# A planner's numbers and 73 of its ranks changed in a chunked-attention, Fourier-mix and MLP kernel; the instructions stay

## The chip, the cores and the metric

The kernel runs on one core of a Trainium2 chip, in one launch. The metric is device microseconds of the whole execution. Before the change the median of three runs is 278.01 us (277.71 to 278.85). The profile is one execution on the same core, read from a hardware trace.

## The reference, cut to what matters

Two parts follow each other. The first is attention in chunks of 32 queries: each chunk sees 8 memory keys, 16 keys to its left, its own 32 and 8 to its right. The second takes the attention's output as rows of 512, adds to each batch the real part of its two-dimensional Fourier transform, normalises the rows, and runs a two-layer MLP over them.

```python
batch, n_heads, seq, head_dim = (4, 8, 768, 64); chunk, left_ctx, right_ctx = (32, 16, 8); n_mem = 8
for c in range(nc):
    k_full = np.concatenate([mem_k, k_ctx], axis=2); v_full = np.concatenate([mem_v, v_ctx], axis=2)
    scores = scale * np.matmul(q_c, k_full.transpose(0, 1, 3, 2))
    a = softmax(scores)
    out[:, :, c_start:c_end] = np.matmul(a, v_full)
...
X = np.fft.fft(np.fft.fft(x, axis=1), axis=2)
u = x + np.real(X)
un = (u - mu) / np.sqrt(var + 1e-06)
ch = np.maximum(un @ w_ch1, 0.0) @ w_ch2          # 512 -> 2048 -> 512
return u + ch
```

## The kernel before, in words

The work is cut into 1,074 tasks. A task is a handful of instructions of one engine: one load, one group of matmuls, one vector operation. Nothing is emitted while the tasks are made. `plan.add` (a method of the class `Plan`) writes down each task's engine, an assumed cost, the tasks it comes after, the buffers it takes and gives back (`take`, `give`), and a rank. Then `plan.order` plays the whole program through as a list scheduler: at each moment each engine gets the ready task of lowest rank. The order in which tasks are placed is the order in which they are emitted, and so the order of every engine's queue on the chip. An engine works through its queue in that order: a task that isn't ready holds all those behind it.

The sixteen units of attention are numbered n = 0 to 15, four per batch, each a pair of heads. A unit loads q and k on GpSimd's DMA queue (`e_load_qk`, line 381 for the first twelve units and line 377 for the last four) and v on SyncE's (`e_load_v`, lines 390, 394 and 399, six DMAs). v is spread into overlapping windows, so its transfers are made of pieces of 256 bytes. Then come the transposes of q and k on TensorE (line 409, "trq" and "trk"), their copies to SBUF (`e_qT` on ScalarE, line 427; `e_kT`, line 452), the scores (line 465, in units 8 and up line 488), the exponentials on ScalarE (lines 475 and 500), the product with v (`e_values`, line 517, "xa" and "xo") and the division on VectorE (`e_norm`, lines 527 and 528). Before v of units 0 to 3 may be loaded, `e_edge_ones` (lines 354 to 359, GpSimd) has to set the edges of its buffer. The transposes need the identity matrix, made on GpSimd (masks.py) and cast on VectorE by `e_idb` (lines 1000 to 1003).

Batch 0 is transformed by `first_fourier` (tasks `g_...`; `g_rows` at line 748, `g_row` at 735), the others by `fourier` (line 589). After them `columns_of` makes the second half of the transform (lines 759 and 780), the sum, the statistics and the normalised rows. The last stage, the MLP, has its first layer at line 897 ("ph"), its relu at 906 and its second layer at 915 (plain form) or 964 (a form with seven products in place of eight, whose partial results VectorE reads at line 969 and whose inputs it combines at line 952). MLP tasks have ranks above 1,000,000: TensorE takes them when nothing else is ready. Task 93, `e_gate` (line 1081), is a one-element copy on GpSimd that waits for v of unit 3; the loads of unit 4 and later stand behind it.

While the first batch is waited for, the planner fills TensorE's gaps with dummy matmuls (line 1024, "idle"): they start once the first scores are placed and end with task 129.

For transfers the planner keeps a model of its own (`share`): a transfer begins `cost * head` after its issue, has a length `moved`, shares the DMA engines with the other queue by the weights `grain`, and its data count as there some time after it ends (`late` and a constant per queue). SyncE places no further task while more than `ROOM` is in its queue. Before the change, the order is the best of 24 plans whose ranks get random additions (`shortest`); tasks below `plan.lead` = 219, which are the first batch's, keep theirs.

Each tile's tag with its `bufs` is a ring of buffers: `rs` (line 857 ff., roots of the variance for the fast form) and `rstd` (line 878 ff., for the plain form) share the ring `rs` of two.

Of the kernel before, what the change touches and what calls it, by code (L numbers as in the profile page):

```python
# [37 lines left out]
class Plan:  # L38
# [10 lines left out]
    ROOM = 2.2  # L49
# [7 lines left out]
    def add(self, engine, cost, emit, after=(), take=(), give=(), rank=None, moved=0.0,  # L57
            loose=False, late=0.0, filler=False, behind=None, lag=0.0, pick=None, grain=0.1, head=1.0):
        t = dict(engine=engine, cost=cost, emit=emit, after=[a for a in after if a is not None],
                 take=take, give=give, rank=len(self.tasks) if rank is None else rank,  # L60
                 moved=moved, done=None, at=None, no=len(self.tasks), loose=loose,
                 late=late, filler=filler, behind=behind, lag=lag, picks=[pick] if pick else [], grain=grain, head=head)
        self.tasks.append(t)
        return t

    def share(self, now):

        left = {q: [list(x) for x in xs_] for q, xs_ in self.flow.items()}
        at = self.seen
        while any(left.values()):  # L70
# [3 lines left out]
            slow = {q: 0.85 if len(live) > 1 and xs_ and xs_[0][0]["grain"] < 0.05 else 1.0  # L74
# [5 lines left out]
            at += step  # L80
            for q, xs_ in left.items():
                if xs_ and xs_[0][2] <= at - step + 1e-9:
                    xs_[0][1] -= step * slow[q] * xs_[0][0]["grain"] / whole
            for q, xs_ in left.items():
# [11 lines left out]
    def shortest(self, tries, spread):  # L96

        free, ranks = dict(self.free), [t["rank"] for t in self.tasks]
        found = None
        for i in list(range(tries)) + [None]:  # L100
            draw = random.Random(found[1] if i is None else i)
            even = (found[1] if i is None else i) == 0
            self.free = dict(free)
            for t, rank in zip(self.tasks, ranks):
                move = draw.gauss(0.0, spread)
                t["rank"] = rank if even or rank < self.lead or rank > 1e5 else rank + move
                t["done"] = t["at"] = None
                for pick in t["picks"]:
                    pick.pop("tag", None)
            placed = self.order()  # L110
            if found is None or self.end < found[0]:
                found = (self.end, i)
        return placed

    def order(self):
        now, idle = 0.0, {}
        self.flow, self.seen, self.full = {}, 0.0, None
# [7 lines left out]
        while any(waiting.values()):  # L125
# [5 lines left out]
            for e, ts_ in waiting.items():  # L131
                if idle.get(e, 0.0) > now or (e == "SP" and self.full and self.full["done"] - self.ROOM > now):
                    continue
                held = False
                for t in ts_:
# [31 lines left out]
                    if t["moved"]:  # L167
# [3 lines left out]
                        if e == "SP" and t["moved"] > 2.5:  # L171
                            self.full = t
# [19 lines left out]
            if not moved:  # L192
# [3 lines left out]
                         + ([self.full["done"] - self.ROOM] if self.full else [])  # L196
# [10 lines left out]
def kernel(  # L207
# [669 lines left out]
    def e_rstd(b):  # L877
        rstd_of[b] = rstd = fpool.tile([P, NST], FP32, tag="rs", bufs=2, name="rstd")
# [116 lines left out]
    t_mkf = add("ACT", 0.2, e_mkf, moved=0.8)  # L995
# [64 lines left out]
    t_gate, LATE, t_flip = None, 1.0, [None]  # L1060
# [4 lines left out]
    def attention(n):  # L1065
# [5 lines left out]
                      take=(("qs", "ks")[i],), moved=3.1 if b >= TURNED else 1.2, grain=0.032 if b >= TURNED else 0.1, late=LATE if b else 2.0,  # L1071
# [4 lines left out]
                 take=("va",), moved=2.6, grain=0.031, head=0.4, late=(0.0, 4.0, LATE, LATE)[b])  # L1076
# [144 lines left out]
    def weights(n):  # L1221
        if n == HP + 1:
            t_w1.extend(add("POOL", 0.7, lambda dt=dt: nc.gpsimd.dma_start(
                w1_sb[:, dt, :], moe_w_ch1[ts(dt, P), :]), moved=2.4, grain=0.32, late=2.0,
                behind=t_mark[0], rank=t_ck[n]["rank"] + 0.1) for dt in range(NDT))
            t_ck[n] = t_w1[-1]
        else:
            t_w2.extend(add("POOL", 0.7, lambda g=g: nc.gpsimd.dma_start(
                w2_sb[:, ts(g, 4), :], w2v[:, ts(g, 4), :]), moved=2.6, late=2.0,
                behind=t_ck[n], rank=t_ck[n]["rank"] + 0.1) for g in (0, 2, 1, 3))  # L1230

    def first_fourier():
        t_rest, t_mid, t_row, pre = {}, {}, {}, {}
        for g in range(2):
            for par in range(2):
                zy = add("DVE", 0.5, lambda par=par, g=g: g_zy(par, g),
                         [t_norm[0, g], t_norm[1, g], t_sines],
                         take=("dn",) if (par, g) == (0, 0) else ())
                if g == 1:
                    w_ = add("DVE", 0.52, lambda par=par: g_w(par), [zy, t_norm[3, 1], pre[par, 1, 0]])  # L1240
# [5 lines left out]
                for ab in range(2):  # L1246
                    pre[par, ab, g] = add("DVE", 0.5,
                                          lambda par=par, ab=ab, g=g: g_ff(par, ab, g, 0),
                                          [zy, t_norm[2, g]],
# [13 lines left out]
            for par in range(2):  # L1263
                for ab in range(2):
# [5 lines left out]
                    else:  # L1270
                        ff = add("DVE", 0.55, lambda par=par, ab=ab: g_both(par, ab),
                                 pre[par, ab, 1][:2], give=("dn",) if (par, ab) == (1, 1) else ())
                    if (par, ab, g) == (0, 0, 1):
# [4 lines left out]
                    lo = add("DVE", 0.48, lambda par=par, ab=ab, g=g: g_lo(par, ab, g), [hi],  # L1278
                             give=("fold",) if end else ())
                    if (par, ab, g) == (0, 0, 0):  # L1280
# [5 lines left out]
                             [lo, t_neg] + ([t_row[g]] if mid_ else []),  # L1286
                             take=(tag,) if g == 0 and not mid_ else (),
                             give=(("hl",), ("hT",))[par] if end else ())
                    if g == 1:
# [8 lines left out]
    def fourier(b):  # L1298
        t_x1 = add("POOL", 1.0, lambda: e_rows_out(b), [t_norm[b * HP + i, 1] for i in range(HP)],
                   moved=2.0)  # L1300
        t_x2[b] = add("SP", 0.6, lambda: e_rows_turn(b), [t_x1], moved=5.5, grain=0.013, loose=True)
        t_xr[b] = add("POOL", 1.0, lambda: e_mirror(b), [t_x2[b]], take=("dn",), moved=2.0, grain=0.16)
# [3 lines left out]
        ff = hi = None  # L1306
        for par in range(2):
# [8 lines left out]
            for ab in range(2):  # L1316
# [5 lines left out]
                lo = add("DVE", 0.96, lambda par=par, ab=ab: e_lo(b, par, ab), [hi],  # L1322
# [269 lines left out]
```

## Time and profile before

| what | value |
|---|---|
| median of 3 runs | 278.01 us |
| span of the profiled execution | 275.7 us |
| its own time less its span | not shown separately; the median is 2.3 us above the span |
| TensorE busy (matmuls) | 258.7 us, 94% of the span |
| VectorE / ScalarE / GpSimd busy | 204.9 / 160.6 / 78.5 us |
| DMA moved | 39.98 MB, mean 145 GB/s |
| granted TensorE clock | 1.000 throughout |

The page gives busy time per engine and a strip of 40 slices of 6.9 us each, with tenths of busy time. A row of the timeline has a start, a duration, the engine, the line, the operation, output and inputs, and a count where like instructions follow each other; in square brackets stands the idle time of the engine just ahead of it and what ended that. Rows of stretches give for each engine the busy time in it, and the busy share of the DMA engines. Dummy matmuls count as busy.

### The profile page before, as it was taken

To read this page: it belongs to the slowest core of one execution; us is meant where nothing else is said; L and a number is where in the kernel's file an instruction comes from. 1 tells how busy PE (TensorE), PEld (TensorE's weight loads), DVE (VectorE), ACT (ScalarE), POOL (GpSimd) and SP (SyncE) were. 2 spreads that over 40 slices of the span, in tenths; PEclk is the share of its full clock that TensorE was granted. 3 is DMA by queue.
4 is the path that set the end of the run, shared out by engine and by line. 5 is a ranking of instruction groups with operands and counts; after the bars stand their busy time and mean duration, and the time that the engine had idled before them with its cause. 6 is when DMAs were issued, how large, how long until landed. Compare 5 with 4: busy or idle time off the path is not lost.

```text
span 275.7 us, 8160 instructions
## 1 busy us (share of the span) xinstructions
PE 258.7 (94%) x3365; PEld 209.8 (76%) x3365; DVE 204.9 (74%) x460; ACT 160.6 (58%) x300; POOL 78.5 (28%) x146
## 2 busy tenths in 40 slices
PE   0489999999999999999999989999999998999995
PEld 0367797888756788658669868888889887888884
DVE  7978999840337999998995997839997996354444
ACT  6888647888555688277646627555373483615150
POOL 8852652350111054045046246001100371000000
PEclk9999999999999999999999999999999999999999
DMA  6999999999997979958989964644960424313152
GB/s 104 203 176 176 193 211 205 198 195 200 174 190 176 204 170 175 212 79 160 241 144 199 183 118 117 123 117 146 132 182 1 95 62 83 111 40 76 64 90 76
DMA packets 116118, 39.98 MB, mean 145 GB/s; under 512 B 104561, under 2 KB 111473, under 8 KB 116081
## 3 DMA queue, kind: packets, MB, share of 16 engines
q1 hardware_dynamic: 93888, 23.54, 47.4%
q0 software_dynamic: 21472, 15.21, 34.8%
q10 hardware_dynamic: 720, 0.72, 0.8%
q8 instruction: 26, 0.43, 0.7%
q14 instruction: 12, 0.09, 0.1%
HBM read 37.36 MB, written 13.37 MB: 184 GB/s over the span
## 4 chain that ended last, share of the span: by engine, by line
PE 80%; DVE 11%; POOL 4%; ACT 2%; issue 1%; POOLq 0%; DVEq 0%
PE ph L897 26%; PE pc L964 14%; PE pc L915 10%; PE ps L589 6%; PE xa L517 5%; PE xo L517 4%; PE pm L759 3%; PE ps L748 3%; DVE S L952 2%; PE sc L465 2%; DVE st L832 2%; DVE xsb L969 2%; PE trk L409 2%; PE idle L1024 1%; PE trq L409 1%; DVE hT L952 1%
## 5 line engine op out<-in xcount | busy, mean ns | idle before, releaser
L897 PE MATMUL ph<-unT,w_sb 128*128 128x256 f16 x768 | 89.6, 273 | 0.0
L897 PEld LDWEIGHTS <-w_sb 128*128 128x128 f16 x768 | 73.7, 98 | 9.3 <-issue 0.3
L906 ACT ACTIVATE hT<-ph 128x512 f16<-128x512 f32 x96 | 56.3, 600 | 39.9 <-PE ph L897 21.1
L964 PEld LDWEIGHTS <-hT 128*128 128x128 f16 x320 | 30.8, 98 | 7.1 <-issue 2.0
L964 PE MATMUL pc<-w_sb,hT 128*128 128x256 f16 x256 | 32.1, 273 | 1.3 <-DVE xsb L969 0.9
L969 DVE TENSOR_TENSOR xsb<-pc,xsb 128x256 f32<-128x256 f32 x57 | 23.7, 420 | 12.6 <-PE pc L964 10.8
L915 PE MATMUL pc<-w_sb,hT 128*128 128x512 f16 x128 | 29.8, 380 | 0.0
L500 ACT ACTIVATE e<-sc,mbias 128x192 f32<-128x192 f32 (+1 forms) x48 | 19.2, 489 | 8.8 <-PE sc L488 8.8
L915 PEld LDWEIGHTS <-hT 128*128 128x128 f16 x128 | 11.8, 98 | 12.9 <-issue 0.4
L952 DVE TENSOR_TENSOR S<-hT 128x768 f16<-128x768 f16 (+1 forms) x16 | 8.5, 533 | 16.1 <-ACT hT L906 15.7
L475 ACT ACTIVATE e<-sc,mbias 128x384 f32<-128x384 f32 x32 | 17.0, 575 | 4.6 <-PE sc L465 4.3
L846 ACT ACTIVATE un<-xsb,rs 128x512 f16<-128x512 f32 x16 | 12.4, 810 | 9.8 <-POOL rs L861 9.8
L964 PE MATMUL pc<-w_t,S 128*128 128x256 f16 x128 | 16.0, 273 | 1.3 <-DVE xsb L969 1.1
L832 DVE BATCH_NORM_STATS2 st<-xsb 128x6 f32<-128x512 f32 x24 | 16.3, 680 | 0.3
L820 POOL TENSOR_TENSOR xsb<-mix,xr 128x512 f32<-128x512 f32 x6 | 8.7, 1459 | 26.6 <-ACT mix L814 26.6
L517 PEld LDWEIGHTS xa<-va,e 128*64 128x64 f32 x384 | 12.9, 142 | 3.8 <-issue 2.7
L601 ACT CAST up<-ps 128x386 f16<-128x386 f32 x16 | 9.7, 606 | 10.4 <-PE ps L589 9.4
L964 PEld LDWEIGHTS <-S 128*128 128x128 f16 x128 | 12.3, 98 | 3.7 <-issue 1.6
L517 PE MATMUL xa<-va,e 128*64 128x65 f32 x384 | 15.2, 230 | 0.0
L517 PE MATMUL xo<-va,e 128*64 128x65 f32 x384 | 14.1, 223 | 0.0
L574 ACT CAST hi<-ff 128x768 f16<-128x768 f32 x12 | 9.7, 829 | 6.3 <-DVE ff L566 6.1
L517 PEld LDWEIGHTS xo<-va,e 128*64 128x64 f32 x384 | 12.6, 138 | 0.5 <-ACT ff L683 0.3
(189 smaller groups left out, 471.9 us busy)
## 6 DMA issues: line engine op xcount, KB each, us to landing
va<-in_v_dram SPq DMA_DIRECT2D x32, 220.0 KB
w_sb<-in_moe_w_ch_dram POOLq DMA_DIRECT2D x8, 512.0 KB, 15.7
out_dram<-xsb SPq DMA_DIRECT2D x12, 256.0 KB
qs<-in_q_dram POOLq DMA_DIRECT2D x12, 192.0 KB, 6.4
ks<-in_k_dram POOLq DMA_DIRECT2D x12, 192.0 KB, 6.9
x_rows<-xsb POOLq DMA_DIRECT2D x3, 768.0 KB, 4.5
xr<-x_back POOLq DMA_DIRECT2D x3, 768.0 KB, 6.0
out_rows<-xsb SPq DMA_DIRECT2D x9, 256.0 KB
```

The source lines that it names most:

```text
L475: nc.scalar.activation(e1[:, :, :, ts(half, 32)], sc[:, :, 0:6, ts(half, 32)], AFT.Exp, bias=mbias[:, half:half + 1], scale=1.0 / math.sqr ...
L500: nc.scalar.activation(to, src, AFT.Exp, bias=mbias[:, half:half + 1], scale=1.0 / math.sqrt(D))
L517: nc.tensor.matmul(xa[64 * half:64 * half + 64, st, hh, 0:65], e1[:, hh, t6, :], v1[:, hh, 6 * g + t6, 0:65], start=True, stop=True)
L589: nc.tensor.matmul(out_[:, sp, :], part[:, ab, sp * 3 + st, c0:c1], tab[:, sp, st, :], start=(st == 0 and i == 0), stop=(st == 2 and i == 1))
L832: nc.vector.bn_stats(st6, xs[b][:, kt, :])
L846: nc.scalar.activation(un, xs[b][:, kt, :], AFT.Identity, bias=rs[:, 1:2], scale=rs[:, 0:1])
L897: nc.tensor.matmul(ph[:, k, :], w1_sb[:, dt, ts(HH * k + i, P)], unT_of[b, j][:, dt, :], start=(dt == 0), stop=(dt == NDT - 1))
L906: nc.scalar.activation(hT_of[b, j][:, :, i, :], ph, AFT.Relu, bias=0.0, scale=1.0 if (b, j) in FAST else -1.0)
L915: nc.tensor.matmul(pc_of[b, j, r], hT_of[b, j][:, k, i, ts(r, P)], w2_sb[:, HH * k + i, :], start=(i + k == 0), stop=(i + k == HH))
L952: nc.vector.tensor_tensor(out_[:, lo:hi], a[:, lo:hi], c[:, lo:hi], op)
L964: nc.tensor.matmul(pc_of[key], a[:, i, :], w[:, i, :], start=(i == 0 and new), stop=(i == HH - 1), skip_group_check=not new)
L969: nc.vector.tensor_tensor(u, pc, u, ALU.add)
```

## The change

No instruction is added or removed; what changes is their order in the queues, and one ring of buffers. The transfer model gets other numbers: for q and k a start of 2.7 times the issue cost, for v 0.9 times a cost of 2.5, the allowance after landing 2.0 (GpSimd's queue) or 1.7 (SyncE's) in place of 2.8 and 1.4, `LATE` 0.3 in place of 1.0, and the same for the stores, the weights and the row turns. SyncE's limit is now on what is left in its queue, weighted by a new number `dense`. Several tasks get further predecessors (`after`), which are listed in the diff only in part. The search over random ranks is gone. `settled` sets the ranks of 73 tasks and plans once. `rs` gets a ring of one and `rstd` a tag of its own with two.

The ranks are by task number. What the numbers mean, for those that are spoken of: 2 the index tables (GpSimd), 6 the casts of the identity (VectorE, from -16.5 to 239.93), 8 the clearing of the k stages' spare rows (GpSimd, line 1007, from 14 to -20.42), 10 the edge ones of v of unit 0 (from -3.5 to 9.2), 16 those of unit 2, 29 and 36 steps of the sine tables, 43 the load of k of unit 0, 58 the load of q of unit 1, 74 and 75 the loads of unit 2, 91 the load of k of unit 3, 92, 221 and 238 the loads of v of units 3, 4 and 5, 126, 128, 131 and 133 the first folds and low parts of batch 0's transform (VectorE, now ahead of all else there), 134 and 138 two of the `g_rows`, 182, 194 and 200 columns of batch 0 (now behind MLP matmuls), 223, 225 and 242 transposes of units 4 and 5 (earlier), 465, 578 and 599 columns of batches 2 and 3 (now among the MLP matmuls), 451 a mix of batch 2, 902 one of VectorE's reads in the MLP, 1073 the store of a last half tile.

```diff
-    ROOM = 2.2
+    ROOM = 1.15
...
-                    t["done"] = at + (2.8 if q == "POOL" else 1.4) + t["late"]
+                    t["done"] = at + (2.0 if q == "POOL" else 1.7) + t["late"]
...
-    def shortest(self, tries, spread):
...
+    def settled(self, moved):
+
+        for no, rank in moved.items():
+            self.tasks[no]["rank"] = rank
+        return self.order()
...
-            rs_of[b] = fpool.tile([P, NST, 2], FP32, tag="rs", bufs=2, name="rs")
+            rs_of[b] = fpool.tile([P, NST, 2], FP32, tag="rs", bufs=1, name="rs")
...
-        rstd_of[b] = rstd = fpool.tile([P, NST], FP32, tag="rs", bufs=2, name="rstd")
+        rstd_of[b] = rstd = fpool.tile([P, NST], FP32, tag="rstd", bufs=2, name="rstd")
...
-    t_gate, LATE, t_flip = None, 1.0, [None]
+    t_gate, LATE, t_flip = None, 0.3, [None]
...
-                      take=(("qs", "ks")[i],), moved=3.1 if b >= TURNED else 1.2, grain=0.032 if b >= TURNED else 0.1, late=LATE if b else 2.0,
+                      take=(("qs", "ks")[i],), moved=2.02 if b >= TURNED else 1.2, grain=0.089 if b >= TURNED else 0.081,
+                      head=1.0 if b >= TURNED else 2.7, late=LATE,
...
-                 take=("va",), moved=2.6, grain=0.031, head=0.4, late=(0.0, 4.0, LATE, LATE)[b])
+                 take=("va",), moved=2.7, grain=0.038, head=0.9, late=LATE, dense=0.84)
...
+    moved = {
+        2: -99.48, 6: 239.93, 8: -20.42, 10: 9.2, 16: 42.33, 18: 31.86, 25: 21.27, 29: 3, 36: 128.29,
+        43: -95.52, 52: -133.92, 58: -97.57, 70: -136.89, 74: -35.68, 75: -26.18, 91: 19.89, 92: 249.51,
+        97: -37.93, 113: -114.22, 126: -128.04, 128: -56.06, 129: 1000618.86, 131: -122.01, 133: -125.37,
+        134: 1000745.25, 138: -56.05, 139: -22.18, 152: 107.39, 159: -88.31, 174: 129.84, 182: 1000572.23,
+        194: 1000645.54, 200: 1000884.49, 201: -152.51, 207: -80.5, 221: 253.87, 223: 135.11, 225: 127.38,
+        230: 1000657.96, 233: 1000721.05, 238: 249.56, 242: 135.12, 244: 1000777.97, 250: 1000530.53,
+        262: 135.01, 269: 1.00059e+06, 275: 396.87, 280: 185.16, 290: -124.87, 318: -83.04, 359: 134.87,
+        360: 147.86, 367: -3.71, 368: 14.55, 375: 1000529.32, 382: 101.94, 393: -60.81, 451: 689.29,
+        465: 1001058.99, 483: 623.83, 532: 1145.25, 544: 292.31, 559: 365.44, 578: 1001262.52,
+        599: 1001418.47, 635: 1000734.08, 636: 297.06, 647: 124.56, 654: 150.33, 675: 1000517.5,
+        822: 804.77, 902: 599.55, 1073: 1412.75,
+    }
     with tc.manual_schedule():
-        for t in plan.shortest(24, 1.5):
+        for t in plan.settled(moved):
             t["emit"]()
```

More of the change, by code (lines that the diff above doesn't have):

```diff
@@ L68, in share @@
         left = {q: [list(x) for x in xs_] for q, xs_ in self.flow.items()}
-        at = self.seen
+        at, self.clear = self.seen, 0.0
+        load = lambda: sum(x[1] * x[0]["dense"] for x in left.get("SP", ()))
         while any(left.values()):
@@ L94, in share @@
             self.flow, self.seen = {}, now
-    def shortest(self, tries, spread):
[L98 to L113, printed above, removed]
+    def settled(self, moved):
+        for no, rank in moved.items():
+            self.tasks[no]["rank"] = rank
+        return self.order()
     def order(self):
         now, idle = 0.0, {}
-        self.flow, self.seen, self.full = {}, 0.0, None
+        self.flow, self.seen, self.clear = {}, 0.0, 0.0
         waiting, since = {}, {}
@@ L131, in order @@
             for e, ts_ in waiting.items():
-                if idle.get(e, 0.0) > now or (e == "SP" and self.full and self.full["done"] - self.ROOM > now):
+                if idle.get(e, 0.0) > now or (e == "SP" and self.clear > now):
                     continue
@@ L1478, in layer2 @@
                           give=(pick(b, j, r, 0),), rank=RELU(len(plan.tasks)))
-                store(b, tiles[r], os_, ("xsb",) if end_b and r == 1 else ())
+                store(b, tiles[r], [os_], ("xsb",) if end_b and r == 1 else ())
             mlp_prev[0] = c2
```

97 lines of the change are left out of this document (53 added, 44 removed).

## The prediction

> **What bounds the kernel now.** I read the page first, then the stretches, then the timeline of each engine up to 33 us. The page, and the dummy matmuls by tile:
>
> ```profile
> span 275.7 us, 8160 instructions
> PE 258.7 (94%) x3365; PEld 209.8 (76%) x3365; DVE 204.9 (74%) x460; ACT 160.6 (58%) x300; POOL 78.5 (28%) x146
> L1024 PE MATMUL idle<-dz x21: 326/326/502, 1.0 to 30.9; 128*128 128x384 bf16 x21
> ```
>
> TensorE is busy 94% of the span, so an order can only win back what is not work. The stretches (start and end, length, then the busy time of each engine; DMA share and GB/s last) say where that lies:
>
> ```profile
> 0.00:31.20 31.20, 20.33 (x440) 15.15 (x442) 26.46 (x75) 23.75 (x40) 18.70 (x51) 1.00 1.03 168
> 31.20:152.00 120.80, 120.77 (x1747) 92.88 (x1747) 91.73 (x186) 80.12 (x147) 39.51 (x63) 1.00 1.14 184
> 160.00:172.00 12.00, 11.02 (x118) 9.37 (x117) 9.89 (x25) 6.70 (x12) 5.85 (x12) 1.00 0.56 116
> 186.00:200.00 14.00, 13.38 (x124) 11.66 (x123) 13.65 (x27) 6.07 (x10) 1.63 (x2) 1.00 0.75 137
> 218.00:232.00 14.00, 12.80 (x116) 10.66 (x115) 12.89 (x30) 7.65 (x15) 9.22 (x15) 1.00 0.45 91
> 272.50:275.70 3.20, 0.00 (x0) 0.00 (x0) 0.42 (x1) 0.00 (x0) 0.00 (x0) 1.00 0.32 112
> ```
>
> Up to 31.2 us TensorE is idle for 10.9 us, and 21 dummies take at least some 5 more. From there to 152 us it misses 0.03 us of 120.8: no order makes this stretch shorter, any order can make it longer. Three later stretches lose 0.98, 0.62 and 1.20, together 2.8. The last store is 3.2. What can be gained is thus in the first 31 us and in those 2.8. The first 31 us, by engine:
>
> ```profile
> 13.86 0.88 PE L409 MATMUL trk<-turn_b,ks 100*64 100x100 bf16 x16
> 17.90 0.55 PE L409 MATMUL trk<-turn_b,ks 100*64 100x100 bf16 x16
> 28.28 0.92 PE L517 MATMUL xa<-va,e 128*64 128x65 f32 x24
> 29.72 0.92 PE L517 MATMUL xo<-va,e 128*64 128x65 f32 x24
> 31.16 0.53 PE L409 MATMUL trq<-ident_b,qs 96*64 96x96 bf16 x16
> 31.89 1.17 PE L735 MATMUL ps<-cosS,mid 128*1 128x193 f16 x12
> ...
> 1.53 0.89 POOL L381 DMA_DIRECT2D qs<-in_q_dram  x1
> 3.75 0.74 POOL masks.py:197 MEMSET ident<- 128x128 f32 x1
> 5.46 0.63 POOL L381 DMA_DIRECT2D ks<-in_k_dram  x1
> 6.14 0.46 POOL L354 TENSOR_SCALAR_AFFINE_SELECT va<-va 32x2 f32<-32x2 f32 x1
> 7.35 0.78 POOL L1030 MEMSET kTb<- 128x384 bf16 x2
> 9.38 1.99 POOL L1007 MEMSET ks<- 4x1024 bf16 x2
> 13.89 0.18 POOL L354 TENSOR_SCALAR_AFFINE_SELECT va<-va 32x2 f32<-32x2 f32 x1
> 25.40 0.18 POOL L1081 COPY gate<-va 1x1 f32<-1x1 f32 x1 [7.54 <-DMA va<-in_v_dram]
> 25.93 0.64 POOL L381 DMA_DIRECT2D qs<-in_q_dram  x1 [0.35 <-PE xa L517]
> ...
> 1.36 0.75 SPq L394 DMA_DIRECT2D va<-in_v_dram  x1
> 22.12 0.31 SPq L399 DMA_DIRECT2D va<-in_mem_v_dram  x1
> 22.53 0.59 SPq L394 DMA_DIRECT2D va<-in_v_dram  x1
> 26.33 0.59 SPq L394 DMA_DIRECT2D va<-in_v_dram  x1
> ...
> 5.55 0.22 DVE L1000 CAST ident_b<-ident 128x128 bf16<-128x128 f32 x1
> 10.41 0.69 DVE L1050 SCALAR_TENSOR_TENSOR tri<-tri 128x512 f32<-128x512 f32 x1
> 11.60 1.25 DVE L452 COPY kTb<-trk 128x1056 bf16<-128x1056 bf16 x1
> 32.20 0.55 DVE L715 TENSOR_TENSOR lo<-ff,hi 128x384 f16<-128x384 f32 x1
> ...
> 14.48 1.06 ACT L475 ACTIVATE e<-sc,mbias 128x384 f32<-128x384 f32 x2
> 28.45 1.05 ACT L475 ACTIVATE e<-sc,mbias 128x384 f32<-128x384 f32 x2 [0.31 <-PE sc L465]
> ...
> L475 ACT ACTIVATE e<-sc,mbias 128x384 f32<-128x384 f32 x16 | 8.4, 572 | 2.4 <-PE sc L465 2.4
> ```
>
> (The last row groups the sixteen exponentials of the first 31.2 us, with the idle time ahead of them, 2.4, behind the second bar.) Two chains run here. SyncE issues v of units 0 to 3 from 1.36 to 22.43 and the last lands at 25.4, where the gate opens. ScalarE runs the exponentials from 14.48 to 29.5. The product of unit 3 starts at 28.28, 2.9 us after its v: now the exponentials set the end, and v has 2.9 us in hand.
>
> **The change, part by part.**
>
> *GpSimd's and SyncE's queues at the start.* By the new ranks GpSimd does the index tables, k of unit 0, q of unit 1, the clearing of the spare rows, q of unit 0, the identity, k of unit 1, q and k of unit 2, the edge ones of unit 1, a clearing of kTb, and only then the edge ones of unit 0, for which v of unit 0 waits; SyncE's later loads stand behind that one. Six loads are 0.89 + 5 x 0.64 = 4.1, the clearing 1.99, the identity 1.1 (3.75 to the next load), kTb 0.4, two sets of edge ones 0.6 to 1.2 each. From 1.53 that makes 10.3 to 11.5 us, where it is 1.36 now. The planner has 1.0 for the clearing and 0.5 for the identity, so it is 1.6 us short here by these rows. SyncE needs 3.7 to 3.8 us for a v with no q or k beside it (22.53 to 26.33) and (22.43 - 1.36)/4 = 5.3 with eight loads beside. v of unit 3 then lands, 3.0 after its last issue as now, between 10.3 + 15.2 + 3.0 = 28.5 and 10.3 + 21.1 + 3.0 = 34.4. Most q and k are done by then, only two loads remain to share with: I take 28.9, 3.5 later than now, nearest to the row without sharing. The product of unit 3 can start there, 0.6 later than now.
>
> *VectorE and ScalarE at the start.* The identity's casts go behind the sine tables, from 5.55 to about 11.1 (10.41 + 0.69); the first transposes go with them. The copy of k of unit 0 is at 11.60 today; 11.1 and two transposes of 0.9 make 13.0, 1.4 later. The exponentials start between 0 and 1.4 later; I take 0.8, since ScalarE's own table work lies between. With three units' q and k already there their gaps (2.4 of the 15.0 from 14.48 to 29.5) can close: they end between 29.5 - 2.4 = 27.1 and 29.5 + 1.4 = 30.9, I take 28.5, with most gaps closed. The second product of unit 3, at 29.72 now, would follow the first at 29.8 at best: no gain there, no loss.
>
> *The folds of batch 0 first.* The first low part is at 32.20 because the division of unit 3's second half and another fold stand ahead of it; with tasks 126 and 128 in front it needs only its own chain, some 0.7 less. The lateness of 0.6 eats this. Against it stands unit 4: its q load waits for the gate, now 25.93, then about 29.4, so its transposes leave 31.16 and TensorE has a dummy there; the work isn't lost, the fold's matmuls take its place. The first part of the program: 0 in sum, between 1.0 gained (v at 28.5, so the second product at 29.4, 0.3 earlier, and 0.7 from the fold) and 6.1 lost (v at 34.4, the first product at 28.28 now).
>
> *Columns of batches 2 and 3, mixes, reads.* These are the losses of 2.8 us; the first and the last of seven waits:
>
> ```profile
> 160.50 1.03 PE L964 MATMUL pc<-w_t,S 128*128 128x256 f16 x8 [0.47 <-DVE xsb L969]
> ...
> 229.63 1.03 PE L964 MATMUL pc<-w_sb,hT 128*128 128x256 f16 x8 [0.43 <-DVE xsb L969]
> ```
>
> Each time a product waits for VectorE, which is between its Fourier work for the next batch and the MLP. Tasks 465, 578, 599 and 451 move that Fourier work behind MLP matmuls, 902 takes a read back. Ends: all 2.8 gone, or the crowd only moves (0, or 1 lost where it meets another product). I take 1.8 gained: two of the three places.
>
> *Changes of kind on TensorE.* A group of eight first-layer matmuls takes less behind its like than behind another kind (rows of the chain that ended last):
>
> ```profile
> 56.42 0.87 PE ph L897 x8
> 71.14 0.98 PE ph L897 x8
> ```
>
> A change of kind costs 0.1 us. The new order has another number of them, which the diff doesn't tell: ten fewer or ten more are 1 us. I take 0.
>
> *Rings and stores.* GpSimd's root for batch 1 loses a wait on `rs`; GpSimd is 28% busy and nobody waits for it there: 0. The last store's rank changes nothing behind the last read: the 3.2 stay.
>
> *The stretch from 31 to 152.* The planner's allowances after a landing shrink by 1.5 us on GpSimd's queue (2.8 + 1.0 become 2.0 + 0.3), so consumers stand closer to their loads. Loads differ widely:
>
> ```profile
> DMA to landing us min/median/max: 4.0/7.1/19.2
> ```
>
> (q, all units). Nothing can be gained; lost can be 0, or 1.5 for each load that comes later than planned, two such at the far end. I take 0.
>
> Sum: 0 - 1.8 = -1.8 against 275.7. The median of the runs stands 2.3 above this span, and I take that as unchanged: 278.0 - 1.8 = 276.2.
>
> *Two rules weighed.* The sixteen transposes take 0.88 at 13.86 and 0.55 at 17.90, with dense matmuls from 13.0. The Trainium skill, "TensorE: Matmul & The Clock Gate", What's actually happening, says the array's clock is halved until about 3.4 us of sustained activity; the rows agree. By that rule a start 1.4 us later keeps it slow 1.4 us longer, and the sum would be worse by an estimated 0.3 to 0.7; the sum goes without it. Likewise an edge select takes 0.46 at 6.14 and 0.18 at 13.89; the Trainium skill, "GPSIMD Engine Reference", Specifications, says that GpSimd shares its SBUF interfaces with VectorE, which speaks for the long end, 11.5, and with it 1.2 more on v.
>
> **The rivals.**
>
> *v becomes the bound (slower).* v of unit 3 lands at 31 or later, since q and k share more than I took or GpSimd's start is at its long end. Each us behind 28.9 then costs one and about a third more, since the gate holds q of units 4 and 5 and the first weights by as much and the matmuls between 33 and 50 us run out of fillers. That is 1.3 us for each us: with all else as forecast it decides from a landing at 28.9 + 3.2/1.3 = 31.3 on. For it: the 8 us that v starts later. Against: the 2.9 in hand. Landing at 32 gives 276.2 + 3.1 + about 1 = 280.3.
>
> *Loads come late in the full stretch (slower).* Two waits of 1.5 us between 31 and 152 where TensorE now has none: 276.2 + 3 = 279.2. For it: DMA share 1.14 there, and smaller allowances. Against: the new model starts a q or k 1.1 us later than the old one (2.7 x 0.66 in place of 0.66), which gives most of the 1.5 back.
>
> *It does nothing that counts (same).* TensorE's work is unchanged and the gaps move: 0 at the start, VectorE's crowd meets other products: 278.0.
>
> **How the numbers follow.** What a measurement here can tell from no change is about 0.5%, 1.4 us. Forecast, faster: 0.42. Same: 0.25. v as bound: 0.20; loads late: 0.13; together slower 0.33. The forecast's own range is 273.2 to 276.6. The low end takes 4.8 us: 1.0 at the start, all 2.8 of the waits, and 1.0 from changes of kind. The high end, 281.5, holds both slower rivals at their prices and a little over a us beyond, short of v at 34.4.
>
> **What would show it.** In the changed profile: SyncE's first v at 10.3 to 11.5; the gate at 28.5 to 30; unit 3's product at 28.5 to 29.5 with TensorE full from 32 at the latest; none or one of the VectorE waits left behind 152; the stretch from 32 to 152 at no idle time. The prediction is wrong if the gate stands past 31, if TensorE has more than a us idle between 33 and 152, or if dummies or idle time up to 31 shrink by over 3 us.

## The result and the profile after

The changed kernel takes 276.91 us, the median of four runs (276.81 to 277.00); the kernel before took 278.02 beside it (277.71 to 278.85). The ratio is 0.9957, with a 95% interval of 0.9941 to 0.9973: 1.1 us faster (0.7 to 1.6), a little less than the 0.5% that the prediction set as its bound for "same", though the whole interval lies below 1. The span of the profiled execution went from 275.7 to 275.1. Wherever a run's span is listed, its time is about 1.7 above it (276.81 and 275.1 here), so the profile of before, at 275.7, belongs to an execution some 0.6 faster than the median, and the two spans understate the gain.

The page of the changed kernel, its first lines:

```profile
span 275.1 us, 8156 instructions
PE 258.2 (94%) x3365; PEld 211.5 (77%) x3365; DVE 206.1 (75%) x460; ACT 160.3 (58%) x300; POOL 80.4 (29%) x146
```

and the stretches that the prediction used (start and end, length, busy time of TensorE, its weight loads, VectorE, ScalarE, GpSimd; then granted clock, DMA share, GB/s):

```profile
0.00:31.20 31.20, 19.38 (x418) 15.21 (x420) 26.93 (x71) 23.80 (x39) 19.12 (x49) 1.00 0.92 153
31.20:152.00 120.80, 120.54 (x1757) 92.61 (x1752) 93.56 (x190) 78.70 (x145) 41.15 (x65) 1.00 1.09 187
160.00:172.00 12.00, 10.95 (x101) 9.38 (x100) 9.31 (x25) 6.18 (x12) 5.95 (x11) 1.00 0.58 110
186.00:200.00 14.00, 13.76 (x129) 12.28 (x129) 13.76 (x27) 6.47 (x11) 1.64 (x2) 1.00 0.70 151
218.00:232.00 14.00, 14.00 (x133) 12.57 (x133) 10.88 (x30) 8.49 (x17) 7.58 (x11) 1.00 0.36 79
```

Two things happened, of opposite sign. Up to 31.2 us TensorE is busy 0.95 less (19.38 for 20.33). Behind 152 us the idle time of the three stretches, 0.98, 0.62 and 1.20 before, is 1.05, 0.24 and 0: 1.5 less, against which a new wait of 0.30 stands outside them. From 31.2 to 152 us 0.26 is idle, for 0.03.

The timeline of the start after, engine by engine (TensorE, SyncE's queue, GpSimd, VectorE, ScalarE):

```profile
12.06 0.88 PE L397 MATMUL trk<-turn_b,ks 100*64 100x100 bf16 x16
21.52 0.88 PE L397 MATMUL trk<-turn_b,ks 100*64 100x100 bf16 x16
30.12 0.92 PE L505 MATMUL xa<-va,e 128*64 128x65 f32 x24
30.87 0.87 PE L505 MATMUL xo<-va,e 128*64 128x65 f32 x24
34.79 0.26 PE L736 MATMUL ps<-cosS,hi 128*128 128x193 f16 x1
...
1.35 0.77 SPq L382 DMA_DIRECT2D va<-in_v_dram  x1
13.59 0.59 SPq L382 DMA_DIRECT2D va<-in_v_dram  x1
...
3.11 2.15 POOL L995 MEMSET ks<- 4x1024 bf16 x2
8.87 1.25 POOL L342 TENSOR_SCALAR_AFFINE_SELECT va<-va 32x2 f32<-32x2 f32 x1
11.62 0.18 POOL L342 TENSOR_SCALAR_AFFINE_SELECT va<-va 32x2 f32<-32x2 f32 x1
13.37 0.20 POOL L336 MEMSET va<- 32x128 f32 x1
25.47 0.41 POOL L1070 COPY gate<-va 1x1 f32<-1x1 f32 x1 [6.19 <-DMA va<-in_v_dram]
...
2.47 1.90 DVE L1030 TENSOR_SCALAR yS<-tri,svS 128x386 f32<-128x386 f32 x3
11.51 0.22 DVE L988 CAST ident_b<-ident 128x128 bf16<-128x128 f32 x1
33.58 1.02 DVE L703 TENSOR_TENSOR lo<-ff,hi 128x384 f16<-128x384 f32 x2
...
8.71 0.69 ACT L1177 ACTIVATE sinS<-rS 128x579 f16<-128x579 f32 x1 [2.29 <-DVE rS L1035]
13.62 0.80 ACT L415 COPY qT<-trq 128x768 bf16<-128x768 bf16 x1 [0.35 <-PE trq L397]
14.44 1.28 ACT L1198 ACT_TABLE_LOAD   x1
15.84 1.04 ACT L463 ACTIVATE e<-sc,mbias 128x384 f32<-128x384 f32 x2
29.70 1.05 ACT L463 ACTIVATE e<-sc,mbias 128x384 f32<-128x384 f32 x2 [0.40 <-PE sc L453]
```

and the same places before, where they don't stand in the prediction:

```profile
33.00 0.26 PE L748 MATMUL ps<-cosS,hi 128*128 128x193 f16 x1
...
2.48 0.18 POOL L354 TENSOR_SCALAR_AFFINE_SELECT va<-va 32x2 f32<-32x2 f32 x1
...
2.47 1.08 DVE L1042 TENSOR_SCALAR yS<-tri,svS 128x386 f32<-128x386 f32 x3
...
12.40 1.28 ACT L1209 ACT_TABLE_LOAD   x1
```

The first row to read is SyncE's: v of unit 0 is still issued at 1.35, and the gate is at 25.47 (25.40 before). Then ScalarE's: the table load ahead of the exponentials stands 2.04 later, the first exponentials 1.36 later, the last 1.25, unit 3's second product 1.15 and the first of the `g_rows` 1.79. In these two profiles the start costs TensorE 1.8 us on its way into batch 0's transform.

TensorE waits for VectorE seven times behind 152 us before the change, and these four times after it:

```profile
161.66 0.39 PE L952 MATMUL pc<-w_t,S 128*128 128x256 f16 x2 [0.59 <-DVE S L940]
162.52 1.03 PE L952 MATMUL pc<-w_t,S 128*128 128x256 f16 x8 [0.47 <-DVE xsb L957]
194.20 1.03 PE L952 MATMUL pc<-w_t,S 128*128 128x256 f16 x8 [0.24 <-DVE xsb L957]
242.60 1.03 PE L952 MATMUL pc<-w_sb,hT 128*128 128x256 f16 x8 [0.30 <-DVE xsb L957]
```

### The profile page after: what moved, and what is told of

It reads as the page before. It is cut to its first block, busy times and chain, and to the rows that moved or that the text cites. A ratio compares the mean times of both kernels' runs of the same rounds, so it can differ in the third digit from the quotient of the medians.

```text
span 275.1 us, 8156 instructions
## 1 busy us (share of the span) xinstructions
PE 258.2 (94%) x3365; PEld 211.5 (77%) x3365; DVE 206.1 (75%) x460; ACT 160.3 (58%) x300; POOL 80.4 (29%) x146
## 3 DMA queue, kind: packets, MB, share of 16 engines
HBM read 37.36 MB, written 13.37 MB: 184 GB/s over the span
## 4 chain that ended last, share of the span: by engine, by line
PE 78%; DVE 13%; ACT 2%; DMA 2%; issue 2%; SPq 1%; POOL 1%; POOLq 0%; DVEq 0%
PE ph L885 25%; PE pc L952 14%; PE pc L903 10%; PE ps L577 6%; PE xa L505 5%; PE xo L505 3%; PE pm L747 3%; PE ps L736 3%; DVE S L940 2%; PE trk L397 2%; PE trq L397 2%; DMA va<-in_mem_v_dram 2%; DVE xsb L516 1%; PE sc L476 1%; PE sc L453 1%
## 5 line engine op out<-in xcount | busy, mean ns | idle before, releaser
L894 ACT ACTIVATE hT<-ph 128x512 f16<-128x512 f32 x96 | 55.5, 600 | 40.9 <-PE ph L885 17.2
L369 POOL DMA_DIRECT2D qs<-in_q_dram x12 | 7.8, 651 | 21.8 <-PE trq L397 18.8
L620 POOL DMA_DIRECT2D xr<-x_back x3 | 2.3, 773 | 37.8 <-ACT up L589 14.2
```

The lines of the kernel that those rows point to most:

```text
L894: nc.scalar.activation(hT_of[b, j][:, :, i, :], ph, AFT.Relu, bias=0.0, scale=1.0 if (b, j) in FAST else -1.0)
```

## The experiments

In the edits, an order is a list of task numbers for one engine; where an experiment writes orders out, only the changed stretch of a list is shown. The kernel before was timed beside every one of them. The profile of each kernel is one execution, and the same order can start differently: `before_late` below has the order of before up to 148 us, but its `g_rows` begin at 34.07, not 33.00, because one q landed later. A us of difference at the start of a single profile therefore proves nothing by itself; the times, over several runs, decide.

**The rings.** The kernel before with the two ring lines of the change and nothing else.

```diff
-            rs_of[b] = fpool.tile([P, NST, 2], FP32, tag="rs", bufs=2, name="rs")
+            rs_of[b] = fpool.tile([P, NST, 2], FP32, tag="rs", bufs=1, name="rs")
...
-        rstd_of[b] = rstd = fpool.tile([P, NST], FP32, tag="rs", bufs=2, name="rstd")
+        rstd_of[b] = rstd = fpool.tile([P, NST], FP32, tag="rstd", bufs=2, name="rstd")
```

> The kernel before with nothing changed but the two rings (rs of one buffer, rstd with a tag of its own). My theory, that the whole difference is in TensorE's queue (2.0 us lost up to 34 us, 2.6 us won between 186 and 245 us): 278.0 us, no change within 0.3. Rival, that the wait of 1.7 us on the shared ring was part of what was won: 277.0 to 277.5.

Measured: 277.82 us beside 277.75, a ratio of 1.0003 (0.9986 to 1.0020). No effect of the rings is shown.

**The late ranks away.** The changed kernel without its eleven ranks from task 451 on, and in a second kernel without the four of 465, 578 and 599 (columns) and 451 (a mix) alone.

```diff
-        ... 451: 689.29,
-        465: 1001058.99, 483: 623.83, 532: 1145.25, 544: 292.31, 559: 365.44, 578: 1001262.52,
-        599: 1001418.47, ...
-        822: 804.77, 902: 599.55, 1073: 1412.75,
```

> The changed kernel without the new ranks of the eleven tasks from 451 on (columns, mix, reads and loads of batches 2 and 3, one store); up to about 148 us the queues are the same. Theory, that these ranks take VectorE's crowd out of the way of the products: the waits of TensorE between 160 and 232 us come back, 276.9 + 1.5 to 2.5 = 278.4 to 279.4 us. Rival, that the waits went because the whole program stands differently by then: 276.9 us.

Measured: 278.91 beside 277.75, a ratio of 1.0051 (1.0034 to 1.0068), 0.0094 or 2.6 us above the changed kernel.

```diff
-        451: 689.29, 465: 1001058.99, 578: 1001262.52, 599: 1001418.47,
```

> The changed kernel without the new ranks of four tasks alone: the columns 465, 578 and 599 and the mix 451. Theory, that columns taken too early give VectorE its crowd: nearly all of the 2.0 us that the eleven ranks are worth comes back, 278.5 us or more, with TensorE's waits at 160 to 172 and 218 to 232 us. Rival, that the read 902, the loads and the others matter: 277 us.

Measured: 279.44 beside 277.51, 1.0064 (1.0044 to 1.0083). Without these four ranks of 73 all of the late gain is gone, though the other seven late ones are in place. Whether the four would win as much without the seven was not run. The timeline shows the price: the waits are at the three places of before again. Around 164 they are longer (1.25 and 0.43, for 0.47 and 0.43), around 230 too (0.99 and 0.43, for 0.21, 0.47 and 0.43), and around 195 shorter (0.23, for 0.19 and 0.43).

```profile
163.44 1.03 PE L952 MATMUL pc<-w_t,S 128*128 128x256 f16 x8 [1.25 <-DVE xsb L957]
...
230.47 1.03 PE L952 MATMUL pc<-w_t,S 128*128 128x256 f16 x8 [0.99 <-DVE xsb L957]
```

**All ranks away.** The new numbers of the transfer model, predecessors and rings, and no rank.

```diff
-        for t in plan.settled(moved):
+        for t in plan.settled({}):
```

> The changed kernel with the new transfer numbers and rings and none of the 73 ranks. Theory, that the new numbers by themselves do not help, since the kernel before had no TensorE wait on a transfer between 31 and 152 us, and that a single plan without a search has more waits on VectorE behind 152 us: 279 to 282 us. Rival, that the transfer numbers are what wins: 277 us or less.

Measured: 281.08 beside 277.51, 1.0126 (1.0100 to 1.0152). The new numbers by themselves, without the search over random ranks that went away with them, give an order 3.5 us slower than before; the ranks bring 4.7 us. Three of its four runs list a mean granted clock of 0.994, so part of this may be the clock (last section).

**The start as before.** The changed kernel with tasks 0 to 112 in the order of before, each in the slots that these tasks have in the changed queues.

```diff
-    'DVE': ... 7, 34, 35, 29, 30, 113, 31, 32, 33, 39, 36, 37, 6, 41, ...
+    'DVE': ... 29, 7, 30, 6, 31, 113, 32, 33, 39, 34, 35, 36, 37, 41, ...
-    'POOL': [2, 43, 58, 8, 42, 4, 59, 74, 75, 13, 24, 10, 21, ...
+    'POOL': [2, 42, 10, 43, 4, 58, 59, 13, 24, 25, 74, 75, 8, 21, ...
```

> The changed kernel, in which the 113 tasks of batch 0's attention and of the tables stand in each engine's queue in the order of the kernel before, in the places that they had; every other task keeps its place. Theory, that the new order of the start costs 2.0 us and the new order behind 186 us wins 2.6: 276.9 - 2.0 = 274.9 us, the first low part of batch 0 at or before 32.2 us. Rival, that the start is where the change wins (the folds first, q and k first) and the lag seen at 34 us is only work put off: 277 to 279 us.

Measured: 276.73 beside 277.75, 0.9965 (0.9951 to 0.9978): nothing won over the changed kernel. The profile says why it isn't a clean test: the planner had put 34 dummies on TensorE for 21. The exponentials do begin early, at 14.61, but the idle time that the rows print ahead of them is 3.4 us for the 1.6 of the changed kernel; the last ones stand at 29.47 (29.70 there) and unit 3's second product at 30.90 all the same. An early first exponential is thus not enough.

**The identity early.** The changed kernel with the identity's casts (task 6) moved ahead of most of the tables.

```diff
-    'DVE': ... 113, 31, 32, 33, 39, 36, 37, 6, 41, ...
+    'DVE': ... 6, 113, 31, 32, 33, 39, 36, 37, 41, ...
```

> The changed kernel with one task moved: VectorE's casts of the identity (task 6) come right behind the cast of the half-precision identity, at about 7.6 us, and no longer behind both tables (11.5 us). All else as changed. Theory, that the start's lag comes from the casts: the first transposes at 8 to 9 us in place of 12.06, the first exponentials 1 us earlier (ScalarE's tables and its table load then stand ahead of them), 1 to 1.5 us of the 2.0 come back: 275.4 to 275.9 us. Rival, that v and its DMA pace the start: 276.9 us.

Measured: 276.34 beside 277.75, 0.9957 (0.9941 to 0.9974), the ratio of the changed kernel. The first transposes came 1.2 earlier (10.87), the first exponentials at 15.76 (15.84). The theory that the identity sets the start falls: when the transposes are done ScalarE is still at its six sines, and its table load comes at 14.36. The move isn't free either. It takes away the 0.35 that the copy of q waits for its transposes after the change, but the casts put VectorE's steps, and with them the first sine, off by as much (9.09 for 8.71).

**The whole start as before.** Tasks 0 to 180 and the dummies in the order of before.

```diff
-    'PE': ... 48, 46, 64, 50, 62, idle, 80, 54, 78, idle, idle, 66, ...
+    'PE': ... 46, 48, 62, 50, idle, 64, idle, 78, 54, 52, 66, ...
```

> The changed kernel with the whole start in the order of the kernel before: tasks 0 to 180 (tables, batch 0's attention, its folds and first transform) and the dummies, each in the slots of its engine's queue that these tasks have in the changed kernel; all other tasks keep their places. The run with 113 tasks moved back began as early as the kernel before (first transposes at 9.13) and was again 2.0 us behind at 34 us, with 13 more dummies and VectorE's folds ahead of the k copy of unit 3. Theory, that the folds' place and the dummies hold the start back: lag at 34 us near 0, and 275.0 us. Rival, that tasks of units 4 and 5 between them, or the loads, hold it: 276.5 to 277 us.

Measured: 276.27 beside 277.51, 0.9952 (0.9935 to 0.9969); the span 274.4, 0.7 less than after. The start is that of before (32.84 for the first of the `g_rows`), but the lead is lost again between 31 and 152 us. The stretch, and a wait of nearly 1 us in it from the timeline:

```profile
31.20:152.00 120.80, 119.42 (x1738) 92.16 (x1738) 92.68 (x187) 79.43 (x149) 40.39 (x65) 1.00 1.11 186
```

```profile
41.04 0.53 PE L472 MATMUL trq<-ident_b,qs 96*64 96x96 bf16 x16 [0.97 <-ACT kTb L515]
```

**Unit 4 as before too.** To that, the loads, transposes and copies of unit 4 (tasks 219 to 235).

```diff
-    'PE': ... 125, 129, 130, 134, 138, 142, 225, 152, 156, 223, 162, ...
+    'PE': ... 223, 125, 129, 130, 134, 138, 142, 152, 156, 162, 168, 174, 225, ...
```

> The changed kernel with the first 181 tasks, the dummies and the loads, transposes and copies of unit 4 in the order of before. start_all lost 1.4 us between 31 and 152, of which a wait of 1.0 at 41 us is the transposes of unit 4 waiting for ScalarE's copy of k. If that wait is the loss, the time is 275.0 to 275.6, a ratio near 0.992. If the middle part's order was planned for a start that is 2 us late and loses the lead at whatever place comes next, the time is that of start_all: 276.2, a ratio of 0.995 to 0.996, with new waits between 41 and 152.

Measured: 276.33 beside 277.98, 0.9940 (0.9927 to 0.9953), not told apart from the kernel before it. The wait of 0.97 is gone, and a like one, again for a copy of k by ScalarE, stands 4 us later. The stretch from 31.2 to 152 has 119.28 us of TensorE work in it, as little as the 119.42 of `start_all`:

```profile
45.06 0.55 PE L472 MATMUL trk<-turn_b,ks 100*64 100x100 bf16 x16 [1.13 <-ACT kTb L515]
```

It looks as if the middle's order was planned for TensorE to arrive later, and an early start runs into it; the two runs fit that, and don't show that nothing else plays a part.

**The late part alone.** The kernel before, its numbers, predecessors and rings, with its own order up to about 148 us on every queue and the changed kernel's order behind that.

```diff
-    'PE': ... 727, 728, 507, 435, 736, 738, 740, 441, 512, 742, 444, 744, ...
+    'PE': ... 727, 507, 728, 435, 736, 441, 512, 738, 444, 448, 740, 742, ...
```

> The kernel before with its own order up to about 148 us on every queue, and the changed kernel's order behind that; numbers, predecessors and rings are those of before. If the late ranks gain by themselves and the start costs by itself, the start's 1.9 us are not paid and the late 2.5 are kept: span 275.7 - 2.5 = 273.2, a time of 275.2 to 275.8 and a ratio near 0.991. If the late gain is only the recovery of a lag that the start made (TensorE arrives 1.9 us later, so VectorE is less late there), then there is nothing to recover here: 277.2 to 278.0, a ratio of 0.998 to 1.001.

Measured: 275.57 beside 277.98, 0.9916 (0.9901 to 0.9931): 2.3 us faster than before (1.9 to 2.8). The late gain doesn't hang on the late start; the first theory holds. It also prices the rest: the changed kernel's order up to 148 us costs 0.9957 - 0.9916 = 0.0041, 1.1 us (about 0.5 to 1.7 by the two intervals).

**The tables alone, and the folds alone.** `before_late` with tasks 0 to 49 (tables, identity, clearing, edge ones, first loads) as in the changed kernel; and `before_late` with tasks 114 to 180 (copies of k, divisions, folds, low parts, first rows) as in it.

```diff
-    'DVE': ... 28, 29, 7, 30, 6, 31, 32, 33, 39, 34, 35, 36, 37, 41, ...
+    'DVE': ... 28, 7, 34, 35, 29, 30, 31, 32, 33, 39, 36, 37, 6, 41, ...
-    'POOL': [2, 42, 10, 43, 4, 58, 59, 13, 24, 25, 74, 75, 8, 21, ...
+    'POOL': [2, 43, 8, 42, 4, 58, 59, 13, 24, 10, 74, 75, 21, ...
```

> before_late with tasks 0 to 49 (tables, casts of the identity, clearing of the spare rows, edge ones, first loads) of the changed kernel. If the sine tables on ScalarE set the first exponentials, these start at 15.5 to 15.9 in place of 14.5, and if the exponentials then carry that to the first g_rows, the time is 1.0 to 1.9 above before_late: 276.6 to 277.5, a ratio of 0.995 to 0.998. If the gaps between the exponentials take it up, and the order of the folds is what costs, the time is that of before_late: 275.3 to 275.9, a ratio of 0.991 to 0.992.

Measured: 278.61 beside 277.75, 1.0041 (1.0026 to 1.0057): 0.0125, or 3.5 us, above `before_late`. It is more than either theory gave. GpSimd's clearing here follows the first k directly, so VectorE's first table step lies beside all of it; the identity comes at 11.91, and on ScalarE the copy of q waits for its transposes with two sines and the table load queued behind it:

```profile
2.47 2.06 POOL L1069 MEMSET ks<- 4x1024 bf16 x2
...
2.47 2.59 DVE L1104 TENSOR_SCALAR yS<-tri,svS 128x386 f32<-128x386 f32 x3
...
14.00 0.80 ACT L489 COPY qT<-trq 128x768 bf16<-128x768 bf16 x1 [1.47 <-PE trq L471]
18.04 1.06 ACT L537 ACTIVATE e<-sc,mbias 128x384 f32<-128x384 f32 x2
...
36.36 0.26 PE L810 MATMUL ps<-cosS,hi 128*128 128x193 f16 x1
```

The exponentials begin 3.55 later than the 14.49 of the next kernel, the `g_rows` 3.38 later than its 32.98: the gaps between the exponentials take up next to nothing.

```diff
-    'DVE': ... 73, 98, 143, 85, 115, 116, 89, 118, 119, 147, 102, 126, 106, 131, 128, 135, ...
+    'DVE': ... 73, 98, 143, 85, 147, 115, 89, 116, 118, 119, 102, 126, 106, 131, 139, 128, ...
```

> before_late with tasks 114 to 180 (copies of k, divisions, folds, low parts and first rows of the first batch) in the order of the changed kernel; the tables and loads stay early. If the folds ahead of unit 3's copy of k hold the last exponentials, the first g_rows come 0.5 to 1.8 later and the time is 0.5 to 1.5 above before_late: 276.1 to 277.0, a ratio of 0.993 to 0.996. If the folds in front gain what the prediction gave them (0.7) the time is 274.9, a ratio of 0.989. If the tables alone are the cost, it is that of before_late: 275.3 to 275.9.

Measured: 275.03 beside 277.75, 0.9906 (0.9890 to 0.9921). Its interval overlaps that of `before_late`, so neither a cost of the folds' order nor a gain of 0.7 is shown. This is the fastest kernel of the study, 2.6 us faster than before and faster than the changed one: old start, old middle, new end. Its timeline, and its second stretch:

```profile
14.49 1.06 ACT L537 ACTIVATE e<-sc,mbias 128x384 f32<-128x384 f32 x2
...
32.98 0.26 PE L810 MATMUL ps<-cosS,hi 128*128 128x193 f16 x1
```

```profile
31.20:152.00 120.80, 120.70 (x1749) 92.79 (x1749) 93.52 (x191) 80.37 (x151) 39.52 (x63) 1.00 1.13 186
```

## Why the prediction was right in sum, and where it was wrong

The sum was -1.8, the times moved by -1.1. It is made of two terms that were both off, in opposite directions: the start and middle, taken as 0, cost 1.1 by the times; the waits, taken as 1.8 gained, gained 2.3. The measured 276.91 stands 0.3 above the forecast's own range, which ends at 276.6, and inside the whole range up to 281.5. That it comes so near is in part luck: the second error makes up for half of the first.

*GpSimd's and SyncE's queues at the start* failed. The step read the planner's predecessor (edge ones before v) as a wait on the chip. It is none: SyncE issues v of unit 0 at 1.35, the edge ones of that buffer are set at 11.62. The row that says so was there before the change: the edge ones at 2.48, the first v at 1.36. Both ends of that step, 10.3 and 11.5, priced something that doesn't happen. GpSimd does hold v, but at another task: the edges of unit 2's buffer are cleared on GpSimd (the row of 13.37), and SyncE issues v of unit 2 right behind it, at 13.59, after 2.6 us in which it issues nothing. Before, it did so at 12.74, behind a like row that ends at 12.72. That lateness of 0.85 is made up by unit 3, whose v is issued at 16.97 for 17.55: the gate stays (25.47, where 28.9 was taken and 25.40 stood before), so the rival in which v becomes the bound had no ground.

*VectorE and ScalarE at the start*: the identity at about 11.1 (11.51 measured) and the copy of k at 13.0 (12.98) held. The exponentials did not: 0.8 later was taken and 1.36 came, and their end, taken as 28.5 with most gaps closed, became 30.75 (29.70 and 1.05). The term was mis-sized because the wrong chain was priced. What holds the exponentials is above all the sine tables: VectorE's steps, then six sines on ScalarE, then the table load. Two rows of the new order make that chain longer: the first table step takes 1.90 for 1.08, and two steps of another table stand ahead of the one that the first sine needs. The first sine starts at 8.71, 1.59 later than the 7.12 of before. Behind the sines the copy of q waits 0.35 for its transposes (the row of 13.62), which is the identity's share. Against that, one copy of q stood between the table load and the first exponentials before, 0.68 from its start to theirs, and stands behind them now: 1.59 + 0.35 - 0.68 are 1.26 of the 1.36. `tables_late` shows that such a lateness can go through in full.

*The folds first*, 0.7 gained, and "0 in sum": the first low part is at 33.58 for 32.20, unit 3's product at 30.12 and 30.87 for 28.9 and 29.8. No run shows the folds' order to be worth anything either way (`folds_late`). The start's price at the first `g_rows` is 1.8 in the profile, inside the range given (1.0 gained to 6.1 lost), by another mechanism. Of the 1.8, 1.36 stand at the first exponentials. The rows say where the rest comes in, though no run isolates it: three dummies (29.53, 0.66 us) now stand in TensorE's queue between the last scores and unit 3's first product, so that this product is 1.84 late, and its division on VectorE, GpSimd's work behind that (32.29 for 30.68) and the first `g_rows` follow 1.6 to 1.8 late.

*Columns, mixes, reads*: right in mechanism and in place ("two of the three places": 186 to 200 in part, 218 to 232 wholly, 160 to 172 not), too small in size: 2.3 (1.9 to 2.8) where 1.8 was taken and 2.8 the far end. The difference is in how the rows were read. The same work in the third place, before and after:

```profile
224.46 1.98 PE L964 MATMUL pc<-w_sb,hT 128*128 128x256 f16 x16
231.62 1.04 PE L897 MATMUL ph<-unT,w_sb 128*128 128x256 f16 x8
...
224.98 1.91 PE L952 MATMUL pc<-w_sb,hT 128*128 128x256 f16 x16
230.78 1.04 PE L885 MATMUL ph<-unT,w_sb 128*128 128x256 f16 x8
```

From the first of these groups to the second it takes 7.16 before and 5.80 after, and the 5.80 hold 0.55 of columns that stood ahead of the place before: 1.9 gained, where the printed idle time gives 1.1 and the prediction counted 1.20. A wait costs more than its idle time. A group of eight reads 1.03 or 1.04 long, but where groups follow each other without a wait they start only 0.87 apart; behind a wait that overlap of 0.16 is lost too, and gaps too short to be printed come on top. Reckoned the same way, the stretch from 167 to 218 us, with the second place in it, gains 0.7, and the new wait at 242.60 loses 0.3: 2.3 in all, as by the times. That at most one wait would be left was wrong: four are. That the four ranks are needed, and the read (902) with the other six does not do it, is shown by `late_columns`.

*Changes of kind*, 0, weren't measured alone. *Rings*: right (1.0003). *The last store*: right, from the start of the last read, at 271.96, to 275.1 are 3.1, and they were 3.2.

*The stretch from 31 to 152*: in the changed kernel it is right, 0.26 idle, and no load is late. But its order is not neutral: with the old start it loses 1.4 us (`start_all`), and with the old order in that place the same start keeps what it has (`before_late`: 0.9916 for 0.9952, 1.0 us; the intervals, 0.9901 to 0.9931 and 0.9935 to 0.9969, just don't overlap).

*The two rules.* The sixteen transposes of k still take 0.88 at 21.52, where they took 0.55 at 17.90. The Trainium skill, "TensorE: Matmul & The Clock Gate", What's actually happening, has the clock halved until some 3.4 us of sustained activity; by that rule a late, sparse start stays slow longer, and the lengths of the rows agree. The clock itself isn't seen: the granted clock of both profiles reads 1.00 throughout the start, and no run shows what the slow rows cost in time. The first edge select of v took 1.25 us at 8.87 and 0.18 at 11.62. The Trainium skill, "GPSIMD Engine Reference", Specifications, has GpSimd and VectorE sharing SBUF interfaces, with contention for VectorE's instructions in two-port modes or with two SBUF inputs; the rows agree, and the prediction applied the rule to the wrong side: what counted was not the longer edge select but the longer VectorE step.

None of the forecast's three signs of failure showed. The gate is not past 31, and TensorE idles for 0.26 us from 31.2 to 152. Up to 31 its idle time grew by 0.95, while the dummies went from 21 to 13 (the other eight came later), from 5.6 to 4.0 us: far from the 3 us less that the third sign asked for.

## What to carry to other kernels

A scheduler's predecessor is not a semaphore: before a moved instruction is priced as a wait, look in the trace whether its follower ever waited for it. A lateness at the start is priced along the chain whose end the next engine needs, here the sines in front of a table load, and not along the first thing that visibly moved. A wait is priced by how much later the work behind it starts, not by the idle time that is printed. And an order is tuned as a whole: a later stretch that was planned behind a late start gives little back when the start is repaired, so keep the part that pays (here four ranks) and put it onto the order whose start is good.

## What the hardware showed beside that

*A VectorE step that meets a GpSimd memset takes nearly three times as long.* The three instructions of the first table step take 0.42 us each before the change, and 1.08 together since they overlap a little, with no large memset beside them. In the changed kernel GpSimd's two memsets start at 3.11, in `tables_late` at 2.47. There the same three take, as shortest, middle and longest:

```profile
L1030 DVE TENSOR_SCALAR yS<-tri,svS x3: 421/455/1189, 2.5 to 3.2; 128x386 f32<-128x386 f32 x3
...
L1104 DVE TENSOR_SCALAR yS<-tri,svS x3: 404/1159/1187, 2.5 to 4.7; 128x386 f32<-128x386 f32 x3
```

One instruction in the first case and two in the second take 1.16 to 1.19, and the others are hardly longer than alone: by these lengths a memset doesn't slow all of them by a share, but holds one at a time, for 0.74 to 0.77. Not every VectorE instruction suffers. The SCALAR_TENSOR_TENSOR steps on 512 columns take 0.75 and 0.69 beside the same memset before the change, and 0.74 and 0.69 without it after. The order of two engines that don't wait for each other is thus part of the price of a move.

*A short stall can be followed by a halved TensorE clock for over 3 us.* In the profile of the kernel without the eleven late ranks, a wait of 1.25 at 161.35 and one of 0.43 are followed by slow matmuls and a granted clock of 0.50. Its timeline, and its stretches of one us (the granted clock is the third column from the end):

```profile
162.60 1.03 PE L952 MATMUL pc<-w_t,S 128*128 128x256 f16 x8 [1.25 <-DVE xsb L957]
164.07 1.73 PE L952 MATMUL pc<-w_sb,hT 128*128 128x256 f16 x8 [0.43 <-DVE hT L940]
```

```profile
164.00:165.00 1.00, 0.93 (x6) 0.71 (x7) 0.96 (x4) 0.00 (x0) 0.00 (x0) 0.63 0.20 40
165.00:166.00 1.00, 1.00 (x6) 0.71 (x5) 0.90 (x3) 0.00 (x0) 0.67 (x2) 0.50 1.00 174
166.00:167.00 1.00, 1.00 (x7) 0.73 (x5) 0.26 (x1) 0.00 (x0) 0.83 (x3) 0.50 0.52 103
167.00:168.00 1.00, 1.00 (x8) 0.75 (x7) 0.46 (x2) 0.76 (x2) 1.00 (x2) 0.66 0.49 94
```

The missing clock sums to 0.37 + 0.50 + 0.50 + 0.34 = 1.7 us, as much as the two waits together. It doesn't come each time: the profiled run lists a mean clock of 0.992, the five others 1.0. The kernel without any ranks shows the same drop behind a wait of 2.21 (0.78, 0.50, 0.50 and 0.52 from 164 on). The kernel without the four ranks has the same two waits of 1.25 and 0.43 and no such drop. The Trainium skill, "TensorE: Matmul & The Clock Gate", What's actually happening, lets the clock fall after an idle window of some 3.4 us, with windows that run free. Here TensorE ran matmuls between the two waits (0.35, 0.40 and 0.64 us of the three before 164), so by that rule a window that is idle in part was enough; why one run has the drop and the other not is open. The idle time that a profile prints is thus a lower bound of what a stall may cost.
